# Block-causal attention, mixture of experts and feed-forward in one kernel: the probabilities of two heads laid side by side before they are transposed

## The chip, the cores and the metric

The kernel runs on one core of a Trainium2 chip, as one program. The metric is device time in microseconds (us) for the whole program. The core has a matrix engine (PE, with its weight loads listed apart as PEld), a vector engine (DVE), an activation engine (ACT), a general engine (POOL) and a queue that mostly issues transfers (SP). Each works through its own instructions in the order in which they are written, and waits on semaphores for the others.

## The reference

Three stages follow each other. In the first, scores are masked so that a row sees its own block of 64 keys and all earlier blocks:

```python
B, H, S, D = (4, 8, 576, 64)
scores = (1.0 / np.sqrt(D)) * np.matmul(q, k.transpose(0, 1, 3, 2))
mask = (pos[:, None] // 64) >= (pos[None, :] // 64)
scores = np.where(mask, scores, -1000000000.0)
attn = np.exp(scores - max);  attn = attn / (sum + 1e-09)
attn_out = np.matmul(attn, v)              # 32 heads of 576 x 64
x = attn_out, heads side by side           # 2304 tokens x 512
# moe: each token goes to the one expert of 8 with the largest logit x @ w_gate
out[mask] = gate_w * (np.maximum(x[mask] @ w1[e], 0) @ w2[e])     # 512 -> 1024 -> 512
# feed-forward: 512 -> 2048 -> 512 with softplus between
return softplus(x @ w_in) @ w_out
```

## The kernel before, in words

Everything is ordered by hand. One long string, `SCHEDULE`, lists short names, and the kernel calls what each name stands for, one after the other; that order is the order of instructions on every engine. A name such as `T10.3` means step `T10` of head pair 3. No scheduler moves anything afterwards.

**Attention** works on 16 head pairs (4 batches of 4 pairs). The 576 rows of a head are cut into chunk 0 (64 rows, 1 block) and chunks 1 to 4 (128 rows each, 2 blocks); chunk c sees 64(2c+1) keys. Per pair these steps occur:

- `Kt`, `Qt` (`prep_pe`, L331): K and Q of both heads are transposed on PE, four 128x128 blocks (`a`) and a fifth for the last 64 rows (`b`). `Kh`, `Qh` (ACT, L343) and `Kl`, `Ql` (DVE, L348) split the result into a high and a low part.
- `S0`, `S1`, `S2` (`scores`, L373): the score products. `m` (`s_max`, DVE, L383 and L381) masks a chunk and finds its extreme, `e` (`s_exp`, ACT, L388) takes the exponential and the row sum. `e41` is chunk 4 of head 1. Score tiles live in PSUM: chunk 4 has the one buffer of pool `ps2`, the others share the three banks of pool `pss` with `Kt` and `Qt`.
- `T` and `h` (`t_pe`, L394, and `t_out`, L399): the probabilities are transposed in 128x128 blocks, four to a bank of pool `ps1` (two banks), and copied to SBUF. `T11` is bank 1 of head 1. A head has 1, 2, 3, 4 and 5 blocks in its chunks, since a chunk's 64(2c+1) keys are padded to 128(c+1) with zeros: 15 blocks a head, 30 a pair, 480 in all. `h0x` and `h1x` are copied by ACT, `h2x` and `h3x` by DVE.
- `V` (`pv`, L409): the product with V, for each block of 128 keys once for each head. The two heads use the left and the right half of PE's columns. The fifth block of keys holds the last 64 rows of V twice, so that it works for either half.
- `F0`, `F1` (`o_out`), `Xa`, `Xb` (L424), `xa`, `xb`, `xo`: the result is turned back to rows, divided by the row sum, and stored; the same product gives the router's logits.

The steps of neighbouring pairs are interleaved: while pair 6 is scored, pair 5 is transposed and multiplied with V, and K and Q of pair 7 are prepared.

**Loads.** `f0`, `f1`, ... load the first batch head by head, `b1.0`, `b1.1`, ... the later batches. All but a few are issued by SP, and so are the stores `xo`, in the order of the string.

**After attention.** From the tenth pair on, DVE also works at the tables that say which token goes to which expert (`er`, the early routing). `wl0` to `wl7` load the first expert's weights, `h1x+0` (ACT) and `l1x+0` (DVE) split its first layer, `g0+0` and `g1+0` (POOL) fetch its tokens. Then come the experts' two layers, and the feed-forward. `lr` and `lg` are the late routing.

Of the kernel before, what the change touches and what calls it, by code (L numbers as in the profile page):

```python
# [54 lines left out]
Kla.1 e31.0 Qla.1 Ktb.1 Qtb.1 u4 e40.0 S1.0 Qhb.1 e01.0 Qlb.1 Khb.1 Klb.1 m30.0 S2.0 u5 m41.0 e30.0 m20.0 e41.0 m00.0
m10.0 e00.0 m21.0 S0.1 e20.0 m11.0 e10.0 e21.0 m40.1 T10.0 e11.0 T20.0 m31.1 h10.0 Kta.2 e40.1 h20.0 T00.0 Qta.2 m01.1
Kha.2 Xr.0 T31.0 h00.0 Kla.2 Qha.2 T21.0 h31.0 e31.1 Ktb.2 Qla.2 Qtb.2 T01.0 Qhb.2 e01.1 Qlb.2 Khb.2 S1.1 h21.0 h01.0
Klb.2 m30.1 S2.1 m41.1 e30.1 m20.1 T11.0 e41.1 m00.1 T30.0 m10.1 e00.1 m21.1 h11.0 m11.1 e20.1 h30.0 V.0 e10.1 e21.1
e11.1 Xr.1 F1.0 S0.2 F0.0 m40.2 T10.1 T20.1 m31.2 h10.1 Kta.3 e40.2 h20.1 T00.1 Qta.3 m01.2 Kha.3 T31.1 h00.1 Kla.3
Xa.0 Qha.3 h31.1 e31.2 Xb.0 Qla.3 T21.1 e01.2 xa.0 T01.1 xb.0 xo.0 b1.10 b1.11 f42 f43 f44 f45 f46 f47 b1.12 b1.13  # L60
b1.14 b1.15 b1.16 b1.17 Ktb.3 Qtb.3 h01.1 h21.1 S1.2 La.0 Qhb.3 Khb.3 Qlb.3 Klb.3 m30.2 S2.2 m41.2 e30.2 m20.2 T11.1
e41.2 m00.2 T30.1 m10.2 e00.2 m21.2 h11.1 m11.2 e20.2 h30.1 V.1 e10.2 e21.2 e11.2 Xr.2 F1.1 S0.3 F0.1 m40.3 T10.2 T20.2
m31.3 h10.2 Kta.4 e40.3 h20.2 T00.2 Qta.4 m01.3 Kha.4 T31.2 h00.2 Kla.4 Xa.1 Qha.4 h31.2 e31.3 Xb.1 Qla.4 T21.2 e01.3
xa.1 T01.2 xb.1 xo.1 Ktb.4 Qtb.4 h01.2 h21.2 S1.3 b2.0 La.1 b2.1 b2.2 b2.3 et Qhb.4 b2.4 b2.5 Khb.4 b2.6 b2.7 Qlb.4
b2.8 b2.9 Klb.4 b2.10 b2.11 m30.3 S2.3 m41.3 e30.3 m20.3 T11.2 e41.3 m00.3 T30.2 m10.3 e00.3 m21.3 h11.2 m11.3 e20.3
h30.2 V.2 e10.3 e21.3 e11.3 Xr.3 F1.2 S0.4 F0.2 m40.4 T10.3 T20.3 m31.4 h10.3 Kta.5 e40.4 h20.3 T00.3 Qta.5 m01.4 Kha.5
T31.3 h00.3 Kla.5 Xa.2 Qha.5 h31.3 e31.4 Xb.2 Qla.5 T21.3 e01.4 xa.2 T01.3 xb.2 xo.2 Ktb.5 Qtb.5 h01.3 h21.3 S1.4 La.2
Qhb.5 Khb.5 Qlb.5 Klb.5 m30.4 S2.4 m41.4 e30.4 m20.4 T11.3 e41.4 m00.4 T30.3 m10.4 e00.4 m21.4 h11.3 m11.4 e20.4 h30.3
V.3 e10.4 e21.4 e11.4 Xr.4 F1.3 S0.5 b2.12 F0.3 b2.13 b2.14 b2.15 b2.16 b2.17 m40.5 T10.4 T20.4 m31.5 h10.4 Kta.6 e40.5
# [1523 lines left out]
```

## Time and profile before

| | |
|---|---|
| median of 3 runs | 888.37 us (887.9 to 888.43) |
| the profiled execution's own time | 888.33 us |
| its span, first to last instruction | 886.6 us |
| PE busy | 869.0 us, 98% |
| PE's weight loads busy | 761.2 us, 86% |
| DVE busy | 671.1 us, 76% |
| ACT busy | 563.0 us, 63% |
| POOL busy | 128.0 us, 14% |

The shares are averages over very different stages. Attention takes roughly the first quarter of the span, the experts somewhat more, the feed-forward the rest. PE's work is pipelined: an instruction's listed length is the time it is under way, and the next begins before it has ended. What one costs in a stream is the distance from start to start.

### The profile page before, as it was taken

How to read it: one execution, taken by the hardware profiler on the slowest of the kernel's cores; microseconds unless marked ns; L12 is line 12 of the kernel's file. 1: busy time of each engine (PE TensorE's matmuls, PEld its weight loads, DVE VectorE, ACT ScalarE, POOL GpSimd, SP SyncE). 2: the span in 40 equal slices, each digit the busy share in tenths (PEclk: the TensorE clock that was granted, in tenths of full speed). 3: DMA queues.
4: the chain of work that ended last, by engine and by line, in shares of the span. 5: the costliest groups of instructions: out<-in, count | busy, mean ns of one | idle time of the engine just before them, and what ended most of it. 6: DMA issues, size and time to landing. Idle time of an engine off the chain costs nothing.

```text
span 886.6 us, 17835 instructions
## 1 busy us (share of the span) xinstructions
PE 869.0 (98%) x6037; PEld 761.2 (86%) x6037; DVE 671.1 (76%) x1627; ACT 563.0 (63%) x1252; POOL 128.0 (14%) x165
## 2 busy tenths in 40 slices
PE   8999999898999999999999999999999999999997
PEld 5788778676899899998998887888888999999997
DVE  6777788887899888765855568667775589897966
ACT  6676776676656667655855688878878734343332
POOL 1010000010022242211310100000000002241502
PEclk9999999999999999999999999999999999999999
DMA  5994734213516378966261567446765893434322
GB/s 122 186 208 83 140 87 142 90 52 122 162 67 211 117 238 282 314 224 224 76 226 48 178 212 229 163 167 219 281 224 202 250 320 109 155 122 141 127 89 96
DMA packets 139349, 148.63 MB, mean 168 GB/s; under 512 B 70895, under 2 KB 96495, under 8 KB 139248
## 3 DMA queue, kind: packets, MB, share of 16 engines
q1 hardware_dynamic: 132960, 132.24, 49.6%
q0 software_dynamic: 4800, 14.70, 4.8%
q8 instruction: 49, 0.80, 0.4%
q10 hardware_dynamic: 1488, 0.46, 0.2%
q14 instruction: 52, 0.43, 0.2%
HBM read 119.56 MB, written 41.43 MB: 182 GB/s over the span
## 4 chain that ended last, share of the span: by engine, by line
PE 63%; DVE 1%; DMA 1%; ACT 0%; issue 0%; SPq 0%; DVEq 0%; ACTq 0%
PE yps L1061 4%; PE yps L1063 3%; PE yps L1062 3%; PE fh L1204 3%; PE fh L1205 3%; PE fh L1203 3%; PE hps L1026 3%; PE hps L1027 3%; PE hps L1028 3%; PE fz L1370 3%; PE fz L1368 3%; PE fz L1369 3%; PE fX L1204 2%; PE fX L1203 2%; PE fX L1205 2%; PE fY L1204 2%
## 5 line engine op out<-in xcount | busy, mean ns | idle before, releaser
L1336 ACT CAST ah<-sum 128x1280 fp32r<-128x1280 f32 (+1 forms) x40 | 46.3, 1157 | 104.2 <-issue 44.7
L388 ACT ACTIVATE P<-s,negm 128x448 f32<-128x448 f32 (+4 forms) x160 | 82.8, 528 | 24.2 <-DVE negm L383 21.2
L1026 PE MATMUL hps<-xh,H1h 128*128 128x256 f32 x320 | 90.8, 284 | 0.0
L1028 PE MATMUL hps<-xh,H1l 128*128 128x256 f32 x320 | 90.5, 283 | 0.0
L1027 PE MATMUL hps<-xl,H1h 128*128 128x256 f32 x320 | 90.5, 283 | 0.0
L982 DVE TENSOR_TENSOR H2l<-R,H2h 128x512 fp32r<-128x512 f32 x96 | 63.7, 686 | 25.7 <-ACT H2h L978 25.7
L383 DVE CUSTOM_DVE_ANT_0 s<-s,mask 128x576 f32<-128x576 f32 (+3 forms) x128 | 69.3, 581 | 14.4 <-PE s L373 13.8
L978 ACT CAST H2h<-R 128x512 fp32r<-128x512 f32 x96 | 57.5, 624 | 29.7 <-PE yps L1062 14.3
L1401 POOL DMA_INDIRECT out_dram<-fos,OI x16 | 46.3, 2892 | 198.3 <-DVE fos L1393 162.5
L1061 PE MATMUL yps<-H2h,hh 128*128 128x512 f32 x176 | 71.5, 407 | 0.4 <-PEq L1533 0.4
L394 PE MATMUL pt<-ident,P 128*128 128x128 f32 x480 | 68.3, 278 | 3.5 <-DVE PT L399 2.5
L1062 PE MATMUL yps<-H2h,hl 128*128 128x512 f32 x176 | 68.8, 391 | 0.0
L1063 PE MATMUL yps<-H2l,hh 128*128 128x512 f32 x176 | 68.7, 391 | 0.0
L982 DVE TENSOR_TENSOR H1l<-R,H1h 128x512 fp32r<-128x512 f32 x96 | 62.2, 684 | 8.3 <-ACT H1h L978 6.2
L1340 DVE TENSOR_TENSOR al<-sum,ah 128x1280 fp32r<-128x1280 f32 (+1 forms) x40 | 54.1, 1352 | 17.4 <-ACT ah L1336 17.3
L978 ACT CAST H1h<-R 128x512 fp32r<-128x512 f32 x96 | 55.5, 623 | 16.0 <-PE hps L1027 10.3
L1026 PEld LDWEIGHTS hps<-xh,H1h 128*128 128x128 f32 x320 | 61.3, 192 | 0.5
L1027 PEld LDWEIGHTS hps<-xl,H1h 128*128 128x128 f32 x320 | 61.3, 192 | 0.3
L1028 PEld LDWEIGHTS hps<-xh,H1l 128*128 128x128 f32 x320 | 61.3, 192 | 0.0
L394 PEld LDWEIGHTS pt<-ident,P 128*128 128x128 f32 x480 | 52.6, 141 | 8.5 <-DVE PT L399 3.3
L409 PE MATMUL o<-PT,vraw 128*64 128x512 f32 (+4 forms) x384 | 59.1, 429 | 0.0
L373 PE MATMUL s<-kZ,qZ 64*128 64x288 f32 (+4 forms) x576 | 55.7, 312 | 3.5 <-DVE kZ L348 2.3
(361 smaller groups left out, 2603.9 us busy)
## 6 DMA issues: line engine op xcount, KB each, us to landing
R<-in_moe_w_dram SPq DMA_DIRECT2D x96, 512.0 KB
gd<-ft SPq DMA_DIRECT2D x64, 256.0 KB
gq<-gd SPq DMA_DIRECT2D x64, 256.0 KB
dbw<-in_moe_w_out_dram SPq DMA_DIRECT2D x32, 256.0 KB
dbl<-in_moe_w_in_dram SPq DMA_DIRECT2D x22, 256.0 KB
yg<-yd SPq DMA_DIRECT2D x4, 1026.0 KB
xd<-xs SPq DMA_DIRECT2D x16, 256.0 KB
wd<-ah SPq DMA_DIRECT2D x4, 896.0 KB
```

Of the source, the lines that this page charges most:

```text
L383: nc.vector.tensor_tensor_reduce(x, x, MASK[:, S - NK[c]:S], scale=1.0, scalar=3.0e38, op0=ALU.add, op1=ALU.min, accum_out=m)
L388: nc.scalar.activation(t[0:n, 0:NK[c]], SC.pop((p, j, c))[0:n], AF.Exp, bias=NM.pop((p, j, c))[0:n], scale=-1.0, accum_out=rs[p % 4][0:n, ...
L394: nc.tensor.transpose(ps[:, o:o + 128], P[p, j, c][:, 128 * kc:128 * kc + 128], ident)
L978: nc.scalar.copy(HW[l, i][0], raw(l, i))
L982: TT(l_, raw(l, i), h.bitcast(F32), op=ALU.subtract)
L1026: mm(a, lhsT=wh, rhs=xh, start=(k == 0), stop=False)
L1027: mm(a, lhsT=wh, rhs=xl, start=False, stop=False)
L1028: mm(a, lhsT=wl, rhs=xh, start=False, stop=(k == 3))
L1061: mm(o, lhsT=h[:, c], rhs=wh, start=(f == 0), stop=False)
L1062: mm(o, lhsT=l[:, c], rhs=wh, start=False, stop=False)
L1063: mm(o, lhsT=h[:, c], rhs=wl, start=False, stop=(f == 7))
L1204: mm(o, lhsT=wh[:, s], rhs=l, start=False, stop=False)
```

## The change

It has three parts.

1. **Probabilities of two heads side by side.** A chunk's tile now holds both heads, head 0's 64(2c+1) keys and then head 1's 64(2c+1), with head 1's blocks of 64 keys in reverse order (`s_exp` writes them so). Together that is 2c+1 whole blocks of 128 for a chunk, with no padding except in chunk 0. The middle one holds the last, unpaired block of 64 keys of both heads. A pair has 1+3+5+7+9 = 25 blocks to transpose. V of odd heads is loaded with the halves of each 128 rows swapped (`swapped`), and the unpaired blocks of V are loaded a second time into a tile `VZ` that has head 0's block in its upper left and head 1's in its lower right quarter and zeros elsewhere (`half_blocks`). `V` begins with four products with `VZ` for chunks 1 to 4, each for both heads in one, and one for chunk 0, and goes on with whole blocks, one for each head.
2. **One block for the last 64 rows of K and Q.** They are loaded into the upper and the lower half of one tile (`last_rows`), and `Ktb` transposes both; `Qtb` is gone. Loads of the last rows fall from 6 a batch to 2, and those of V grow in number (a later batch is 30 transfers where it was 18).
3. **A new order** of the whole attention part and of what lies beside it: the early routing, the first expert's loads, its token fetches and its conversions. From `V.15` on the two strings are the same, word for word.

The bank of the early routing moves from `ps2` to `ps1`, and the warm-up products at the start are 19 where they were 18.

```diff
-BANK = [
-    [(0, 1, 0), (0, 2, 128), (0, 3, 256), (0, 4, 384)],
...
-BW = [512, 512, 512, 320]
-NPB, PTB = 4, 4
+BANK = {
+    "00": [(0, 1, 0), (0, 2, 0), (0, 3, 0), (0, 4, 0)],
+    "10": [(1, 2, 0), (1, 3, 0), (1, 4, 0), (3, 4, 0)],
+    "20": [(2, 3, 0), (2, 4, 0), (2, 3, 1), (2, 4, 1)],
+    "21": [(c, c, None) for c in range(1, 5)],
+    "30": [(0, 0, None)],
+}
+for n in "01":
+    BANK[n + "1"] = [(kc, c, 1) for kc, c, _ in BANK[n + "0"]]
+NPB = 2
...
+    def last_rows(b, h0, nh):
+        t, i = raw[b, "k"], slice(h0, h0 + nh)
+        return [(t[r:r + 64, 4, i], x[b, i, 512:576, :].rearrange("h p d -> p h d")) for r, x in ((0, k), (64, q))]
+
+    def half_blocks(b, h):
+        o = slice(64 * (h % 2), 64 * (h % 2) + 64)
+        return VZ[b % 2][o, :, h // 2, o], v[b, h].rearrange("(n p) d -> p n d", p=64)[:, 0:9:2, :]
+
+    def swapped(b, h):
+        x = v[b, h].rearrange("(n p) d -> p n d", p=64)
+        return [(raw[b, "v"][64 * i:64 * i + 64, :, h], x[:, 1 - i:8:2]) for i in range(2)]
...
     def s_exp(p, j, c):
         n = SPAN[c][1]
-        t = P[p, j, c] = PB[(2 * p + j) % NPB][c]
-        nc.scalar.activation(t[0:n, 0:NK[c]], SC.pop((p, j, c))[0:n], AF.Exp, ...
+        t, x = PB[p % NPB][c][0:n, NK[c] * j:NK[c] * j + NK[c]], SC.pop((p, j, c))[0:n]
+        if j and c:
+            t, x = (a.rearrange("p (b k) -> p b k", k=64) for a in (t, x))
+            t = t[:, ::-1, :]
+        nc.scalar.activation(t, x, AF.Exp, ...
...
+    def t_pe(p, n):
+        if n == "30":
+            ps = PS[p, "E"] = pss.tile([128, 512], F32, tag="s", name="pt0")
+        else:
+            ps = PS[p, n] = ps1.tile([128, 512], F32, tag="ps1", name="pt")
+        for i, (kc, c, j) in enumerate(BANK[n]):
+            a = NK[c] + 64 + 128 * (c - 1 - kc) if j else 128 * kc
+            nc.tensor.transpose(ps[:, 128 * i:128 * i + 128], PB[p % NPB][c][:, a:a + 128], ident)
...
+        w = 64 if n == "30" else 512
+        (nc.scalar.copy if n in ("00", "01", "10") else nc.vector.tensor_copy)(t, ps[:, 0:w])
...
     def pv(p):
         b, hp = divmod(p, H // 2)
         o = PS[p, "o"] = pso.tile([128, 512], F32, tag="o", name="o")
-        o0 = PS[p, "o0"] = pss.tile([128, 512], F32, tag="s", name="o0")[:, 0:64]
-
-        for a, w, c, i, f in ((0, 512, 0, 0, 0), (0, 512, 1, 1, 0), (128, 384, 2, 2, 0), (384, 128, 4, 2, 384), (256, 256, 3, 3, 0), (None, 64, 0, 3, 256)):
+        o0 = PS[p, "o0"] = PS.pop((p, "E"))[:, 128:192]
+        for c in range(1, 5):
+            mm(o[:, 128 * c - 128:128 * c], lhsT=VZ[b % 2][:, c, hp], rhs=PT[p, "21"][:, 128 * c - 128:128 * c], start=c == 1, stop=False)
+        mm(o0, lhsT=VZ[b % 2][:, 0, hp], rhs=PT[p, "30"], start=True, stop=True)
+        for n, f, a, w, c in (("0", 0, 0, 512, 0), ("1", 0, 128, 384, 1), ("1", 384, 384, 128, 3), ("20", 0, 256, 256, 2)):
             for j in range(2):
-                out = (o0 if a is None else o[:, a:a + w])[64 * j:64 * j + 64]
-                mm(out, lhsT=raw[b, "v"][:, c, 2 * hp + j], rhs=PT[p, j, i][:, f:f + w], ...
+                r = PT[p, n][:, f + 256 * j:f + 256 * j + w] if n == "20" else PT[p, f"{n}{j}"][:, f:f + w]
+                mm(o[64 * j:64 * j + 64, a:a + w], lhsT=raw[b, "v"][:, c, 2 * hp + j], rhs=r, start=False, stop=c == 2)
...
-Xr.5 F1.4 S0.6 F0.4 m40.6 T10.5 T20.5 m31.6 h10.5 Kta.7 e40.6 h20.5 T00.5 Qta.7 m01.6 Kha.7 T31.5 h00.5 Kla.7 Xa.4
...
+e41.5 e10.5 S0.6 T20.5 F1.4 m40.6 F0.4 e21.5 Qta.7 e40.6 h20.5 Qha.7 T00.5 Kta.7 h00.5 Xa.4 Xb.4 m01.6 m31.6 T10.5
```

The new order is best seen on the engines. On PE, at the end of a steady period (pair 6), the last transposes and the product with V stand like this before; `pt` are transposes (P_0 and P_1 are tiles of probabilities, one set for a head), `o<-PT` products with V, 64x512 for one head.

```order
L394 MATMUL pt<-ident,P_1_129 128x128
L394 MATMUL pt<-ident,P_1_130 128x128
L394 MATMUL pt<-ident,P_1_131 128x128
L394 MATMUL pt<-ident,P_1_132 128x128
L394 MATMUL pt<-ident,P_0_126 128x128
L394 MATMUL pt<-ident,P_0_127 128x128
L394 MATMUL pt<-ident,P_0_123 128x128
L409 MATMUL o<-PT_1616,vraw 64x512
L409 MATMUL o<-PT_1652,vraw 64x512
L409 MATMUL o<-PT_1588,vraw 64x512
L409 MATMUL o<-PT_1714,vraw 64x512
L409 MATMUL o<-PT_1596,vraw 64x384
```

And now, at the same place (one set of P tiles for a pair):

```order
L420 MATMUL pt<-ident,P_0_126 128x128
L420 MATMUL pt<-ident,P_0_127 128x128
L420 MATMUL pt_1621<-ident,P_0_123 128x128
L433 MATMUL o<-PT_1603,VZ_134 128x128 x4
L434 MATMUL pt_1621<-PT_1625,VZ_134 128x64
L438 MATMUL o<-PT_1526,vraw 64x512
L438 MATMUL o<-PT_1619,vraw 64x512
L438 MATMUL o<-PT_1583,vraw 64x384
L438 MATMUL o<-PT_1623,vraw 64x384
L438 MATMUL o<-PT_1583,vraw 64x128
L438 MATMUL o<-PT_1623,vraw 64x128
L438 MATMUL o<-PT_1512,vraw 64x256 x2
```

Before, the four rows of P_1 at the top give PT_1714, which the fourth product reads; now five products with `VZ` stand between the last transposes and the first product with a half of PE's columns.

On ACT, at the same place of the same pair, these rows stood before (`P<-s` are exponentials, PT copies of transposed probabilities, xT the copy of V's result):

```order
L388 ACTIVATE P_2_136,rs_122<-s,negm 128x448
L388 ACTIVATE P_3_142,rs_122<-s_1657,negm 128x576
L388 ACTIVATE P_2_133,rs_122<-s,negm 64x64
L399 COPY PT_1714<-pt 128x512
L388 ACTIVATE P_2_135,rs_122<-s,negm 128x320
L388 ACTIVATE P_2_134,rs_122<-s,negm 128x192
L388 ACTIVATE P_3_140,rs_122<-s,negm 128x320
L388 ACTIVATE P_3_139,rs_122<-s,negm 128x192
L415 COPY xT_117<-o 128x512
```

And now:

```order
L410 ACTIVATE P_1_131,rs_122<-s,negm 128x448
L410 ACTIVATE P_1_128,rs_122<-s,negm 64x64
L426 COPY PT_1619<-pt 128x512
L410 ACTIVATE P_1_130,rs_122<-s,negm 128x320
L410 ACTIVATE P_1_129,rs_122<-s,negm 128x3x64
L410 ACTIVATE P_1_132,rs_122<-s_1567,negm 128x9x64
L410 ACTIVATE P_1_129,rs_122<-s,negm 128x192
L444 COPY xT_117<-o 128x512
L410 ACTIVATE P_1_130,rs_122<-s,negm 128x5x64
L410 ACTIVATE P_0_127,rs_119<-s_1657,negm 128x576
```

The exponential of chunk 4 of head 1 (128x576, now 128x9x64) was second and is sixth, the copy of PT is behind two exponentials where it was behind three, and the last exponential of the pair now stands behind the copy of V's result.

## Rows read from the trace of the kernel before

**Rows 1.** The page: the span, and each engine's busy time, share and instructions.

```profile
span 886.6 us, 17835 instructions
PE 869.0 (98%) x6037; PEld 761.2 (86%) x6037; DVE 671.1 (76%) x1627; ACT 563.0 (63%) x1252; POOL 128.0 (14%) x165
```

**Rows 2.** Busy time by stretch: length, busy us of each engine, granted clock, DMA.

```profile
24.80:128.90 104.10, 103.86 (x881) 85.10 (x880) 78.68 (x269) 73.52 (x233) 6.38 (x29) 1.00 0.75 147
76.90:89.90 13.00, 13.00 (x112) 10.60 (x110) 9.80 (x34) 9.20 (x30) 0.27 (x1) 1.00 0.12 30
128.90:221.50 92.60, 86.20 (x729) 67.99 (x727) 76.48 (x288) 64.08 (x197) 5.44 (x14) 1.00 0.30 97
142.70:171.30 28.60, 26.05 (x233) 20.87 (x232) 26.64 (x117) 18.75 (x59) 1.07 (x4) 1.00 0.39 132
221.50:886.60 665.10, 658.35 (x4282) 593.97 (x4280) 500.31 (x1024) 410.54 (x780) 112.07 (x85) 1.00 0.56 182
```

**Rows 3.** PE's instructions in time, pair 5: start, length, what, count.

```profile
84.49 1.39 PE L424 MATMUL psx<-xrhs,xT 128*128 128x144 f32 x10
85.72 1.04 PE L394 MATMUL pt<-ident,P 128*128 128x128 f32 x8
86.59 0.27 PE L331 MATMUL psT<-ident,kraw 128*128 128x128 f32 x1
86.90 2.24 PE L373 MATMUL s<-kZ,qZ 64*128 64x448 f32 x24
89.08 0.98 PE L394 MATMUL pt<-ident,P 128*128 128x128 f32 x7
89.99 3.88 PE L409 MATMUL o<-PT,vraw 128*64 128x512 f32 x24
93.79 0.48 PE L373 MATMUL s<-kZ,qZ 64*128 64x288 f32 x2
```

**Rows 4.** The product with V in time, ACT and PE's weight loads beside it.

```profile
90.47 1.02 PE L409 MATMUL o<-PT,vraw 128*64 128x512 f32 x3
90.76 0.57 ACT L399 COPY PT<-pt 128x512 f32<-128x512 f32 x1
90.90 1.13 PE L409 MATMUL o<-PT,vraw 128*64 128x512 f32 x3
91.38 0.19 PEld L409 LDWEIGHTS o<-PT,vraw 128*64 128x64 f32 x3 [0.34 <-ACT PT L399]
```

**Rows 5.** PE's groups by line, 60 to 140 us: busy, mean ns, idle before.

```profile
L394 PE MATMUL pt<-ident,P 128*128 128x128 f32 x188 | 26.6, 278 | 0.0
```

**Rows 6.** DVE's and ACT's groups by line, 63 to 141 us.

```profile
L399 DVE COPY PT<-pt 128x512 f32<-128x512 f32 x12 | 8.2, 681 | 0.0
L399 DVE COPY PT<-pt 128x320 f32<-128x320 f32 x12 | 5.8, 483 | 0.0
L413 DVE COPY xT<-o 128x64 f32<-128x64 f32 x6 | 1.3, 224 | 1.5 <-PE o L409 1.5
L388 ACT ACTIVATE P<-s,negm 128x192 f32<-128x192 f32 x12 | 5.0, 415 | 0.0
```

**Rows 7.** DVE in time: first and last step around seven extremes, and a small step.

```profile
93.39 0.22 DVE L429 RECIPROCAL rinv<-rinv 128x10 f32<-128x10 f32 x1
...
101.24 0.63 DVE L383 CUSTOM_DVE_ANT_0 s<-s,mask 128x448 f32<-128x448 f32 x1 [0.22 <-PE s L373]
...
104.32 0.49 DVE L399 COPY PT<-pt 128x320 f32<-128x320 f32 x1
```

**Rows 8.** ACT's groups by form, later stages: a read of every second element, a plain one.

```profile
L937 ACT ACTIVATE cvh<-dbl 128x256 f32<-128x256 f32 x18 | 7.2, 435 | 3.5 <-DMA dbl<-in_moe_w_in_dram 2.2 <-DVE cvl L938 1.4
L1213 ACT ACTIVATE ft<-fh 128x256 f32<-128x256 f32 x7 | 2.7, 381 | 2.9 <-PE fh L1205 1.8 <-DMA gd<-ft 1.0
```

**Rows 9.** SP's issues and ACT's first conversions in time.

```profile
43.76 6.36 SPq L291 DMA_DIRECT2D vraw<-in_v_dram  x6
193.81 1.14 ACT L978 CAST H1h<-R 128x512 fp32r<-128x512 f32 x2 [0.65 <-PE psT L331]
```

More of the change, by code (lines that the diff above doesn't have):

```diff
@@ L55 @@
[L55 to L69, printed above, removed]
@@ L286, in load_raw @@
             t = raw[b, nm]
+            g = slice(0, H, 2) if nm == "v" else slice(0, H)
             for c in range(4):
-                l.append((t[:, c], src[nm][b, :, 128 * c:128 * c + 128, :].rearrange("h p d -> p h d")))
-            for r in (0, 64):
-                l.append((t[r:r + 64, 4], src[nm][b, :, 512:576, :].rearrange("h p d -> p h d")))
+                l.append((t[:, c, g], src[nm][b, g, 128 * c:128 * c + 128, :].rearrange("h p d -> p h d")))
+            if nm == "k":
+                l += last_rows(b, 0, H)
+        for h in range(1, H, 2):
+            l += swapped(b, h)
+        l += [half_blocks(b, h) for h in range(H)]
         return [lambda o=o, i=i: nc.sync.dma_start(o, i) for o, i in l]
@@ L300, in attention @@
     rs = [const.tile([128, 5, 2], F32, name=f"rs{i}") for i in range(4)]
-    PB = [[const.tile([128, 128 * (c + 1)], F32, name=f"P{c}_{i}") for c in range(5)] for i in range(NPB)]
+    PB = [[const.tile([128, 2 * NK[c]], F32, name=f"P{c}_{i}") for c in range(5)] for i in range(NPB)]
+    VZ = [x.tile([128, 5, H // 2, 128], F32, name=f"VZ{i}") for i, x in enumerate((rawp, const))]
     def fill(t, v):
@@ L313, in attention @@
     start += [fillg(t[:, 576:640], 0.0) for t in xTp] + [fillg(t, 1.0) for t in rs]
-    for s in PB:
-        start += [fillg(s[0], 0.0)] + [fillg(s[c][:, 128 * c + 64:], 0.0) for c in range(1, 5)]
+    start += [fillg(s[0], 0.0) for s in PB]
+    start += [fillg(t, 0.0) for t in VZ]
     P, PS, PT, SC, NM, XS, Z = {}, {}, {}, {}, {}, {}, {}
@@ L321, in prep_pe @@
         b, hp = divmod(p, H // 2)
-        if part == "a":
-            ps = PS[p, nm] = pss.tile([128, 512], F32, tag="s", name="psT")
-            cs, off = range(4), 0
-        else:
-            if nm == "k":
-                PS[p, "4"] = pss.tile([128, 512], F32, tag="s", name="psT4")
-            ps, cs, off = PS[p, "4"], [4], {"k": 0, "q": 128}[nm] - 512
-        for c in cs:
+        ps = PS[p, nm if part == "a" else "4"] = pss.tile([128, 512], F32, tag="s", name="psT")
+        for i, c in enumerate(range(4) if part == "a" else [4]):
             t = raw[b, nm][:, c, 2 * hp:2 * hp + 2, :].rearrange("p h d -> p (h d)")
-            nc.tensor.transpose(ps[:, off + 128 * c:off + 128 * c + 128], t, ident)
+            nc.tensor.transpose(ps[:, 128 * i:128 * i + 128], t, ident)
     def prep_src(p, nm, part):
```

435 lines of the change are left out of this document (224 added, 211 removed), and 3 rows, old and new, of the table BANK.

## The prediction

> **What bounds the kernel now.** First the page: PE is busy 869.0 of the span of 886.6 us [rows 1]. Such a share says that PE is the engine to look at, not how much of its time is work, since the listed lengths overlap. So next the busy times by stretch, one for each stage [rows 2]. From the first product with V (24.8 us) to the ninth (128.9) eight pairs take 104.1 us, 13.0 each, and PE is idle for 0.24 us in all. A steady pair takes 13.00 us with PE busy 13.00, DVE 9.80 and ACT 9.20. In the next seven pairs (128.9 to 221.5) PE is idle for 6.4 of 92.6 us while DVE, which now has the routing beside attention, is busy 76.48; in its densest part, 142.7 to 171.3, it is busy 26.64 of 28.6, or 93%. From 221.5 on the two programs are the same; PE is idle there for 6.8 of 665.1 us. The granted clock is 1.00 (2.4 GHz) in all of them. So where the change acts, PE sets the pace, and for seven pairs DVE sets it with PE.
>
> Then PE's instructions in time, for what one costs [rows 3]. Eight transposes start at 85.72 and the next instruction at 86.59: 0.109 us each. The product with V starts at 89.99 and the scores behind it at 93.79: 3.80 us. Is that all work? One head's passes over 512 columns start 0.43 us apart (90.47, 90.90) [rows 4], there are two for each product, and the heads run side by side in the two halves. A head has 512+512+384+128+256+64 = 1856 columns, so 1856/512 x 2 x 0.43 = 3.12 us would do. The rest is mostly a wait: PE's weight loads stand idle until 91.38 behind ACT's copy of a PT tile, which runs from 90.76 to 91.33 [rows 4]. That is the copy behind three exponentials in the order on ACT. PE counts as busy meanwhile, since the other head's half is streaming: no idle time shows it.
>
> **The change, step by step.**
>
> *Transposes.* A pair loses 5 of 30 blocks of P, and one of its ten blocks of K and Q: 6 x 16 = 96. At 0.109 us each that is 0.65 us a pair, 10.5 us in all.
>
> The Trainium skill (TensorE: Matmul & The Clock Gate, Part 4: PE-mode transpose) puts a 128x128 transpose at about 275 ns in a kernel's context, and the trace's mean of one is indeed 278 ns [rows 5]. By that figure 96 would be 26.4 us. But 188 of them are busy for 26.6 us together [rows 5], half of what the mean would make, and in a stream the start-to-start price is what a removed one gives back.
>
> *The product with V.* The four `VZ` products have 128 columns in two passes, with weights over the whole array, which the trace has in two forms: transposes at 0.109, and `psx` with 144 columns at (85.72 - 84.49)/10 = 0.123 [rows 3]. Eight passes are 0.87 to 0.98; I take 0.9, nearer the transposes, which have the same width. Chunk 0's product is two passes of 64 columns, 0.05 each by columns, 0.109 if the weight load decides: 0.2 at most, taken. The whole blocks are 1280 columns a head: 1280/512 x 2 x 0.43 = 2.15. Together 3.25. The columns are as many as before; what goes is the wait: the last copies now have the 1.1 us of `VZ` products to be ready in, ACT's copy stands behind two exponentials, not three, and is needed second. Saved: 3.80 - 3.25 = 0.55 a pair (0 if a wait of the same size takes its place, 0.68 at most).
>
> *DVE and ACT.* DVE copies three tiles of 512 and one of 64 for two of 512 and two of 320: with 0.68, 0.22 and 0.48 [rows 6], -0.06 a pair. ACT loses one copy of 512. Four exponentials a pair are now written with blocks of 64 in reverse. No row has that; between nothing and the 0.05 us by which a read of every second element exceeds a plain one (435 against 381 ns [rows 8]): at most 0.2 a pair, on an engine with 3.8 us to spare.
>
> *The new order.* The next pair's `S0` needs the banks freed by the last exponentials. Between the end of `S1` and that `S0` PE does `S2` (half of 86.90 to 89.08: 1.09), nine transposes (0.98), the product with V (3.25) and a changeover (0.15): 5.5 us. In the same time DVE does the seven extremes of `S1` and `S2` (101.24 to 104.32 when they come in one run: 3.1 [rows 7]), two copies of 512 (1.36), one of 64 (0.22), and the two small steps of the reciprocal (0.2 each by [rows 7]): 5.1, and then ACT the last exponential, 0.42 [rows 6]: 5.5. That is a tie. Before, chunk 4's extreme came early and there was slack. So there may be a new wait of 0 to 0.5 us a pair at `S0`; I take 0.15, because most of ACT's and DVE's steps overlap at their ends.
>
> *Pairs 0 to 8.* Eight intervals, each shorter by 0.65 + 0.55 - 0.15 = 1.05: 8.4 us (5.2 without any gain at V, 9.6 without the new wait).
>
> *Pairs 9 to 15.* Here PE's own work would fall to 86.2 - 7 x 1.2 = 77.8 us, but DVE keeps 76.48 - 0.4 = 76.1. At the 93% that it reached in its densest part that takes 81.8 us; if only the transposes are felt, 92.6 - 7 x 0.65 = 88.0. The routing's steps are spread over more pairs now, which speaks for the lower figure, and the waits between the engines for the upper: I take 84.5, a gain of 8.1 (4.6 to 10.8).
>
> *The seam.* The first expert's conversions ran from 193.81 [rows 9] and are read only after the last product with V at 221.5: more than 20 us of cover. In the new order they are spread over the last two and a half pairs, the last some 10 us ahead of that point. Costed at nothing; if the cover were gone, one conversion would be about 0.6 us late.
>
> *Start.* The first scores now stand behind the second pair's K and Q, whose loads come later, but SP issues five transfers fewer before the first product with V, at about 1.06 us each (six in 6.36 us [rows 9]). Costed at 0, with 1 us either way. Behind `V.15` its own 0.5 is gained once more.
>
> *Sum.* 8.4 + 8.1 + 0.5 = 17.0. The profiled execution took 888.33 us, practically the median of the runs shown (888.37): 871.3 us.
>
> **Rivals.**
>
> *The wait moves.* The tie above goes the wrong way and `S0` waits 0.5 us in each pair, so that only the transposes are felt: 8 x 0.65 + 4 = 9.2, 879 us. For it: DVE and ACT have no slack left there. Against it: PE waits for an exponential nowhere in the steady pairs now.
>
> *Everything is had.* No new wait, and the routing's pairs at DVE's densest: 9.6 + 10.8 + 1 = 21.4, 867 us. Against it: 93% was reached over two pairs, not seven.
>
> *Slower: the chain through DVE and ACT becomes the bound.* In one pair it runs from `S0` through chunk 4's extreme and exponential, `Xa` and `Xb`, `S1`, DVE's 5.1 us and the last exponential back to `S0`. I count about 11.7 us for it, as for PE. From 13.0 on it costs more than the change gives, so its links would have to be 1.3 us longer than counted: a quarter of a microsecond at each of five hand-overs between engines. At 13.3 in 15 intervals, 892 us. Against it: every link but one is in today's order too, in 13.0 us with 3.2 us of DVE idle.
>
> *V comes late.* A later batch has 12 transfers more. Batch 1's last V load is issued by 50.1 [rows 9], and its first product starts at 76.9 [rows 2], 72.5 after the change. At 1.06 us each, 12 more end at 62.9: ten us to spare, nothing lost. At 2 us each and one after the other they would end 1.7 us late, three batches, 5 us: 876 us.
>
> The Trainium skill (SBUF - State Buffer, The DMA setup-cost knee) is on this rival's side: it gives every transfer a fixed cost of about 2 us and warns of many small ones. The trace has six in 6.36 us, so much of such a cost overlaps here.
>
> **How the numbers follow.** The forecast 0.55, the moved wait 0.24, everything 0.10, V late 0.04, slower 0.05, no change 0.02 (a wait that happens to eat it all). About 0.2% is what a measurement of this kernel tells from no change. Faster by more than that: 0.55 + 0.24 + 0.10 + 0.04 = 0.93; within it 0.02; slower 0.05. The range takes in the forecast, the moved wait and everything, with the bounds of the terms (17.0 may be 8.8 to 21.9): 866 to 880.
>
> **What would show it.** In the changed kernel's trace: 400 transposes of P where there were 480, still 0.109 apart; the product with V 3.2 to 3.4 us from its first start to the next scores, with no weight load waiting for a PT copy; steady pairs of 11.9 to 12.1 us with PE busy throughout; the seven pairs from the ninth product with V to the last in 82 to 88 us, DVE busy about 90%; the first product with V between 24 and 26 us; and 665 us from the last one on. Wrong would make it: PE idle before `S0` for an exponential (the moved wait), exponentials of chunk 4 in reverse much over 0.74 us, or PE idle before `V` for a load.

## The result, and the profile after

The changed kernel takes 877.78 us (median of 4 runs, 877.16 to 878.41) against 888.34 us for the kernel before: ratio 0.9882, 95% interval 0.9868 to 0.9896. That is faster by 10.6 us where 17 were forecast; the time lies inside the range. The profiled execution took 877.16 us, its span is 875.5 us.

The busy times by stretch of the changed kernel, cut at the same places as [rows 2] (first, fifth, sixth, ninth and last product with V); the columns are those of [rows 2]:

```profile
24.63:124.50 99.87, 99.33 (x849) 80.06 (x849) 76.90 (x266) 71.46 (x224) 6.40 (x29) 1.00 0.68 140
74.73:87.18 12.45, 12.37 (x107) 9.96 (x107) 9.62 (x34) 9.04 (x28) 0.27 (x1) 1.00 0.39 91
124.50:209.99 85.49, 83.12 (x703) 65.85 (x702) 75.32 (x287) 62.48 (x187) 6.08 (x14) 1.00 0.38 112
209.99:875.50 665.51, 658.06 (x4284) 594.40 (x4282) 500.17 (x1027) 410.76 (x780) 105.01 (x85) 1.00 0.56 184
```

The span fell by 11.1 us: 0.2 ahead of the first product with V, 104.10 - 99.87 = 4.2 in pairs 0 to 8, 92.60 - 85.49 = 7.1 in pairs 9 to 15, and 0.4 went back behind the last product. The seven pairs came out nearly as forecast (84.5). The eight steady ones did not: a pair takes 12.45 us, 0.55 less than before and not 1.05.

PE's instructions in time through one steady pair of the changed kernel (start, length, what, count), to be held against [rows 3]:

```profile
74.73 1.06 PE L433 MATMUL o<-PT,VZ 128*128 128x128 f32 x8
75.63 0.33 PE L434 MATMUL pt<-PT,VZ 128*128 128x64 f32 x2
75.89 2.37 PE L438 MATMUL o<-PT,vraw 128*64 128x512 f32 x16
78.20 1.13 PE L392 MATMUL s<-kZ,qZ 64*128 64x288 f32 x12
79.25 0.66 PE L420 MATMUL pt<-ident,P 128*128 128x128 f32 x4
...
81.15 1.49 PE L453 MATMUL psx<-xrhs,xT 128*128 128x144 f32 x10
82.48 1.04 PE L420 MATMUL pt<-ident,P 128*128 128x128 f32 x8
83.35 0.27 PE L350 MATMUL psT<-ident,kraw 128*128 128x128 f32 x1
83.55 2.22 PE L392 MATMUL s<-kZ,qZ 64*128 64x448 f32 x24
85.70 1.64 PE L420 MATMUL pt<-ident,P 128*128 128x128 f32 x9
87.18 1.06 PE L433 MATMUL o<-PT,VZ 128*128 128x128 f32 x8
```

Cut into pieces from start to start, with those of before out of [rows 3] (`S0` stands 13.00 ahead of 93.79 there, at 80.79):

| piece of a steady pair | before | after | difference |
|---|---|---|---|
| `S0` to `psx` (`S0` and 23, now 16 transposes) | 3.70 | 2.95 | -0.75 |
| `psx` | 1.23 | 1.33 | +0.10 |
| to `S1` (10, now 9 transposes) | 1.18 | 1.07 | -0.11 |
| `S1` and `S2` | 2.18 | 2.15 | -0.03 |
| to `V` (7, now 9 transposes) | 0.91 | 1.48 | +0.57 |
| `V` | 3.80 | 3.47 | -0.33 |
| sum | 13.00 | 12.45 | -0.55 |

Seven transposes left the piece from `S0` to `psx`, and it fell by what they cost, 7 x 0.109 = 0.76 us: in the kernel before PE's weight loads follow each other there without a gap. In the last piece it is otherwise. Nine transposes at 0.109 us are 0.98; between `S2` and `V` they take 1.48. PE's weight loads there say what they wait for (start, length, what, count; in brackets the idle time before and what ended it):

```profile
85.70 0.42 PEld L420 LDWEIGHTS pt<-ident,P 128*128 128x128 f32 x4
86.43 0.42 PEld L420 LDWEIGHTS pt<-ident,P 128*128 128x128 f32 x4 [0.31 <-DVE PT L426]
87.01 0.14 PEld L420 LDWEIGHTS pt<-ident,P 128*128 128x128 f32 x1 [0.16 <-ACT P L410]
```

The second four wait until DVE has copied the bank of four pairs of blocks (`h21`), the last one, chunk 0's, until ACT's exponentials have freed its bank. Now DVE and ACT of the same pair:

```profile
79.41 0.77 DVE L402 CUSTOM_DVE_ANT_0 s<-s,mask 128x576 f32<-128x576 f32 x1 [2.10 <-PE s L392]
80.26 0.74 ACT L410 ACTIVATE P<-s,negm 128x576 f32<-128x576 f32 x1 [0.79 <-DVE negm L402]
...
82.68 0.56 DVE L471 TENSOR_TENSOR xs<-psx,rinv 128x384 f32<-128x384 f32 x1 [0.27 <-PE psx L453]
...
84.89 0.22 DVE L400 TENSOR_REDUCE negm<-s 64x1 f32<-64x64 f32 x1 [0.25 <-PE s L392]
85.14 0.63 DVE L402 CUSTOM_DVE_ANT_0 s<-s,mask 128x448 f32<-128x448 f32 x1
...
85.95 0.64 ACT L410 ACTIVATE P<-s,negm 128x448 f32<-128x448 f32 x1 [1.47 <-DVE negm L402]
...
86.58 0.29 ACT L410 ACTIVATE P<-s,negm 64x64 f32<-64x64 f32 x1
```

Read with PE's rows, this is a ring. `S0` (78.20), chunk 4's extreme (79.41) and exponential (80.26), which frees the two banks for `psx` (81.15), DVE's multiplications of `psx` (82.68 to 83.78), which free them for head 1's half of `S1`, chunk 0's and chunk 3's extremes (84.89, 85.14), their exponentials (85.95, 86.58), chunk 0's transpose (87.01), `V` (87.18), and 3.47 us later the next `S0`. Each begins within about 0.2 us of the end of the one before. PE stands still at several places of that ring; the ring nowhere. That was the theory to be tested. Its rival: PE's own work fills the 12.45 us and the prices were wrong.

### The profile page after: what moved, and what is told of

Same layout as the page of the kernel before. It is cut to its first block, busy times and chain, and to the rows that moved or that the text cites. A ratio compares the mean times of both kernels' runs of the same rounds, so it can differ in the third digit from the quotient of the medians.

```text
span 875.5 us, 17767 instructions
## 1 busy us (share of the span) xinstructions
PE 861.2 (98%) x5974; PEld 754.4 (86%) x5974; DVE 667.5 (76%) x1627; ACT 559.6 (64%) x1236; POOL 124.2 (14%) x149
## 4 chain that ended last, share of the span: by engine, by line
PE 65%; DMA 1%; ACT 0%; SPq 0%; issue 0%; DVE 0%; DVEq 0%; ACTq 0%
PE yps L1090 4%; PE yps L1092 4%; PE yps L1091 3%; PE fh L1233 3%; PE fh L1234 3%; PE fh L1232 3%; PE hps L1056 3%; PE hps L1057 3%; PE hps L1055 3%; PE fz L1399 3%; PE fz L1397 3%; PE fz L1398 3%; PE fX L1233 2%; PE fX L1234 2%; PE fX L1232 2%; PE fY L1233 2%
## 5 line engine op out<-in xcount | busy, mean ns | idle before, releaser
L410 ACT ACTIVATE P<-s,negm 128x192 f32<-128x192 f32 (+4 forms) x160 | 83.6, 526 | 39.1 <-DVE negm L402 33.8
L402 DVE CUSTOM_DVE_ANT_0 s<-s,mask 128x576 f32<-128x576 f32 (+3 forms) x128 | 70.1, 569 | 26.4 <-PE s L392 23.5
L1430 POOL DMA_INDIRECT out_dram<-fos,OI x16 | 41.0, 2561 | 204.8 <-DVE fos L1422 166.5
L420 PE MATMUL pt<-ident,P 128*128 128x128 f32 x400 | 61.1, 281 | 2.1 <-DVE PT L426 0.8
L392 PEld LDWEIGHTS s<-kZ,qZ 64*128 64x128 f32 x576 | 47.3, 185 | 14.0 <-ACT P L410 5.5
L420 PEld LDWEIGHTS pt<-ident,P 128*128 128x128 f32 x400 | 44.3, 141 | 11.1 <-DVE PT L426 4.4
```

The costliest lines, as they stand in the source:

```text
L392: mm(o, lhsT=a, rhs=b, start=first, stop=last)
L402: nc.vector.tensor_tensor_reduce(x, x, MASK[:, S - NK[c]:S], scale=1.0, scalar=3.0e38, op0=ALU.add, op1=ALU.min, accum_out=m)
L410: nc.scalar.activation(t, x, AF.Exp, bias=NM.pop((p, j, c))[0:n], scale=-1.0, accum_out=rs[p % 4][0:n, c, j:j + 1])
L420: nc.tensor.transpose(ps[:, 128 * i:128 * i + 128], PB[p % NPB][c][:, a:a + 128], ident)
```

## Experiments

Each was timed beside the kernel before, whose median was 888.1 to 888.2 us there. All but the columns of time are from the profiled execution; the code behind the last product with V is the same in all, yet takes 663.7 to 669.3 us from that product to the end, so that small effects are read from the stretches and not from the total.

| run | median, us | ratio to before, 95% | first `V` | steady pair | pairs 0 to 8 | pairs 9 to 15 |
|---|---|---|---|---|---|---|
| before | 888.34 | | 24.80 | 13.00 | 104.10 | 92.60 |
| changed | 877.78 | 0.9868 to 0.9896 | 24.63 | 12.45 | 99.87 | 85.49 |
| e1 six more | 880.02 | 0.9887 to 0.9918 | 25.97 | 12.52 | 100.74 | 85.61 |
| e2 two more | 877.35 | 0.9862 to 0.9892 | 24.89 | 12.44 | 100.06 | 85.14 |
| e3 VZ last | 888.23 | 0.9991 to 1.0009 | 24.89 | 13.17 | 106.09 | 89.41 |
| e4 old places | 895.27 | 1.0060 to 1.0087 | 24.47 | 12.45 | 99.88 | 97.76 |
| e5 swap | 875.94 | 0.9850 to 0.9879 | 24.33 | 12.43 | 99.85 | 85.19 |
| e6 swap, copy on ACT | 876.05 | 0.9846 to 0.9875 | 24.98 | 12.44 | 99.85 | 84.50 |
| e7 old places behind `S0` | 888.17 | 0.9993 to 1.0011 | 24.35 | 12.45 | 99.89 | 96.52 |
| e8 before, early copy | 885.65 | 0.9969 to 0.9990 | 24.93 | 12.72 | 102.27 | 91.67 |
| e9 chunk 3 first | 873.48 | 0.9825 to 0.9852 | 24.25 | 12.26 | 98.57 | 84.22 |
| e10 and copy on ACT | 876.14 | 0.9856 to 0.9887 | 25.01 | 12.27 | 98.61 | 83.68 |
| e11 before, one block | 887.92 | 0.9994 to 1.0012 | 24.30 | 13.00 | 104.17 | 92.50 |
| e12 before, chunk 3 first | 885.93 | 0.9965 to 0.9986 | 24.89 | 12.83 | 103.13 | 91.54 |

**What the transposes were worth (e1, e2, e11).** e1 puts as many back as the change took away; they write the same blocks to the same places once more. e2 does it in bank 11 alone.

```diff
-        for i, (kc, c, j) in enumerate(BANK[n]):
+        for i, (kc, c, j) in [x for x in enumerate(BANK[n]) for _ in range(2 if n in ('20', '10', '11') and x[0] < 2 else 1)]:
```

> The changed kernel, but in three of a pair's seven banks (20, 10 and 11) the first two blocks are transposed twice into the same place: six transposes more a pair, as many as the change took away, 96 in all. At 0.109 us each that is 0.65 us a pair and 10.5 us. If PE alone sets the pace of the changed kernel, the steady pair goes from 12.45 to 13.1 us and the total rises by 10 to 10.5 us. If the steady pair is set by hand-overs from DVE and ACT (the changed kernel shows PE held up before the second bank of four transposes, before chunk 0's transpose and before psx, together about half a microsecond a pair), most of the six disappear in these waits: 12.5 to 12.8 us a pair, 1.5 to 5 us in total.

> The changed kernel, but in bank 11 alone, just ahead of the bank for which PE waits for DVE's copy, the first two blocks are transposed twice: 32 transposes more, 0.22 us a pair. If the wait is real, they are hidden in it: steady pair 12.45 to 12.5, total within 1 us of the changed kernel. If PE sets the pace: 12.67 us a pair and 3.5 us in total.

e1: 0.07 us in the steady pair, where 0.65 would be work; 2.2 us in total. Of these 1.3 stand ahead of the first product with V and are not the transposes' doing: in e1's trace the first of them starts at 19.03, and the delay is there by then, since PE ran at a granted clock of 0.50 from 15 to 18 us (1.00 in the changed kernel). The one of e1's four runs with a mean granted clock of 1.000 took 878.18 us. e2: nothing (12.44). In e1 the waits have gone into the transposes, as PE's instructions show: eleven of them behind `S2` take hardly longer than nine did, and `psx` and `S1` run without their waits.

```profile
83.18 1.39 PE L453 MATMUL psx<-xrhs,xT 128*128 128x144 f32 x10
84.41 1.25 PE L420 MATMUL pt<-ident,P 128*128 128x128 f32 x10
...
85.70 2.01 PE L392 MATMUL s<-kZ,qZ 64*128 64x448 f32 x24
87.64 1.68 PE L420 MATMUL pt<-ident,P 128*128 128x128 f32 x11
89.16 0.40 PE L433 MATMUL o<-PT,VZ 128*128 128x128 f32 x2
```

`psx` 1.23, `S1` and `S2` 1.94 (2.15 in the changed kernel), the last transposes 1.52. So the changed kernel has almost 0.6 us of room on PE in each steady pair.

e11 makes the second part of the change alone, in the kernel before: K's last 64 rows in the upper and Q's in the lower half of one tile, one transpose for both.

```diff
-        for r in (0, 64):
-            l.append((t[r:r + 64, 4, h0:h0 + nh], src[nm][0, h0:h0 + nh, 512:576, :].rearrange("h p d -> p h d")))
+        for r, x in ((0, nm), (64, "q" if nm == "k" else nm)):
+            l.append((t[r:r + 64, 4, h0:h0 + nh], src[x][0, h0:h0 + nh, 512:576, :].rearrange("h p d -> p h d")))
...
+        if nm + part == "qb":
+            return
```

> The kernel before with the second part of the change alone: the last 64 rows of K and Q in one block, one transpose less a pair (16 in all) and four transfers less a batch. By the start-to-start price of 0.109 us a steady pair goes from 13.00 to 12.89, the total down by 1.7 us (pairs 9 to 15 may keep theirs). By the mean duration of one, 0.278 us, it would be 4.4 us. If before, too, is held by hand-overs in the steady pair, nothing: within 0.5 us.

Nothing, neither in the steady pair nor in total. The transpose is gone, and what stands behind it has become longer by as much:

```profile
86.08 0.27 PE L335 MATMUL psT<-ident,kraw 128*128 128x128 f32 x1
86.28 2.35 PE L377 MATMUL s<-kZ,qZ 64*128 64x448 f32 x24
88.56 0.98 PE L398 MATMUL pt<-ident,P 128*128 128x128 f32 x7
```

0.20 us for the block of K instead of 0.31 for two [rows 3], then 2.28 for `S1` and `S2` instead of 2.18: `S1` waits for DVE to read `psx` in any case. So the kernel before had waits of PE too, though its PE is busy 13.00 us of 13.00 [rows 2]. This transpose stood behind `psx`, in front of such a wait; none was taken from the piece between `S0` and `psx` alone, where PE has no wait.

**The product with V (e3, e8).** e3 puts the products with `VZ` and chunk 0's behind the whole blocks.

```diff
-        for c in range(1, 5):
-            mm(o[:, 128 * c - 128:128 * c], lhsT=VZ[b % 2][:, c, hp], ..., start=c == 1, stop=False)
-        mm(o0, lhsT=VZ[b % 2][:, 0, hp], rhs=PT[p, "30"], start=True, stop=True)
         for n, f, a, w, c in (("0", 0, 0, 512, 0), ...
...
-                mm(o[64 * j:64 * j + 64, a:a + w], ..., start=False, stop=c == 2)
+                mm(o[64 * j:64 * j + 64, a:a + w], ..., start=n == "0", stop=False)
+        for c in range(1, 5):
+            mm(o[:, 128 * c - 128:128 * c], lhsT=VZ[b % 2][:, c, hp], ..., start=False, stop=c == 4)
+        mm(o0, lhsT=VZ[b % 2][:, 0, hp], rhs=PT[p, "30"], start=True, stop=True)
```

> The changed kernel with the products of V in another order: the whole blocks of 128 keys first, the four products with VZ and chunk 0's last. Same instructions, no cover for the last copies of PT. If the products with VZ are what hides ACT's last copy, V grows by 0.4 to 0.6 us a pair (3.47 to 3.9 to 4.1) and the total by 6 to 9 us. If the order within V does not matter, because the steady pair waits elsewhere anyway, less than 1.5 us.

`V` grows from 3.47 to 4.10 us (91.47 to 95.57 below) and the pair from 12.45 to 13.17. The whole blocks take 2.85 us where they took 2.31; PE's weight loads stand idle for 0.35 us among them, until 92.02, behind ACT's copy of a PT tile. All of the change's gain is gone: 888.23 us is the time of before. That it is the same time is chance: pairs 0 to 8 are slower than before (106.09 for 104.10), pairs 9 to 15 still faster (89.41 for 92.60).

```profile
91.47 2.91 PE L435 MATMUL o<-PT,vraw 128*64 128x512 f32 x16
94.32 1.16 PE L437 MATMUL o<-PT,VZ 128*128 128x128 f32 x8
95.31 0.33 PE L438 MATMUL pt<-PT,VZ 128*128 128x64 f32 x2
95.57 0.67 PE L392 MATMUL s<-kZ,qZ 64*128 64x288 f32 x5
```

e8 shortens the wait in the kernel before: ACT's copy of bank 1 of head 1 goes one exponential up.

```diff
-... T11.7 e41.8 m00.8 T30.7 m10.8 e00.8 m21.8 h11.7 m11.8 e20.8 h30.7 V.7
+... T11.7 e41.8 m00.8 T30.7 m10.8 h11.7 e00.8 m21.8 m11.8 e20.8 h30.7 V.7
```

> The kernel before, but ACT's copy of bank 1 of head 1 (the PT tile for which the product with V waits in the middle) stands ahead of chunk 0's exponential, behind two exponentials where it stood behind three. Nothing else changes. If the product with V of before holds a wait of half a microsecond for that copy, which no idle time shows, its length goes from 3.80 to 3.45 to 3.6 us and the total down by 2.5 to 5 us. If the length is work, or another copy is as late, less than 1 us.

`V` 3.52 us, 0.28 less than before, and the pair 12.72, 0.28 less:

```profile
89.05 3.59 PE L409 MATMUL o<-PT,vraw 128*64 128x512 f32 x24
92.57 1.12 PE L373 MATMUL s<-kZ,qZ 64*128 64x288 f32 x12
```

The hidden wait in `V` was real, and what is taken from `V` comes back in full: `V` is a link of the ring in the kernel before.

**The other links (e5, e6, e9, e10, e12).** e5 swaps two neighbours on DVE, from pair 3 on:

```diff
-... Klb.8 h10.6 m00.7 m30.7 S2.7 h21.6 T11.6 ...
+... Klb.8 h10.6 m30.7 m00.7 S2.7 h21.6 T11.6 ...
```

e6 does the same and takes `h21` to ACT:

```diff
-... Klb.8 h10.6 m00.7 m30.7 S2.7 h21.6 T11.6 ...
+... Klb.8 h10.6 h21.6 m30.7 m00.7 S2.7 T11.6 ...
...
-        (nc.scalar.copy if n in ("00", "01", "10") else ...
+        (nc.scalar.copy if n in ("00", "01", "10", "21") else ...
```

> The changed kernel, but from pair 3 on DVE takes the extreme of chunk 3 of head 0 ahead of that of chunk 0 (two neighbours on one engine change places, nothing else). Theory: a steady pair is a closed chain without slack, S0, chunk 4's extreme and exponential, psx, its two multiplications on DVE, S1, the extremes of chunks 0 and 3, their exponentials, chunk 0's transpose, V, S0: its links add up to the 12.45 us. The swap takes the 0.25 us of chunk 0's extreme out of the chain, but PE's wait for DVE's copy of bank 21 then ends last, 0.10 to 0.15 us earlier than now: steady pair 12.30 to 12.37, total 1 to 2 us down. If PE's own work is what fills the 12.45 us: no change (within 0.5 us).

> As the swap of chunk 3's and chunk 0's extremes, and the copy of bank 21 is done by ACT, right behind that of bank 10, and no longer by DVE. Neither PE's wait for that copy nor chunk 0's extreme is then in the way of the last transposes. Theory of the closed chain: 0.2 to 0.3 us a pair, steady pair 12.15 to 12.25, and DVE has 0.68 us less in each of the routing's pairs: total 3 to 5 us below the changed kernel. If another link takes over at once: less than 1 us.

Both failed to move the steady pair (12.43, 12.44). ACT and DVE of e5 show why:

```profile
84.59 0.63 DVE L402 CUSTOM_DVE_ANT_0 s<-s,mask 128x448 f32<-128x448 f32 x1 [0.26 <-PE s L392]
...
85.31 0.22 DVE L400 TENSOR_REDUCE negm<-s 64x1 f32<-64x64 f32 x1
...
85.65 0.63 ACT L410 ACTIVATE P<-s,negm 128x448 f32<-128x448 f32 x1 [1.47 <-DVE negm L400]
```

The exponential of chunk 3 now waits for chunk 0's extreme (L400), the later of the two: they share one score tile. The link is as long as it was, so neither run speaks against the ring. e6 removes PE's wait for `h21` all the same, and chunk 0's transpose then waits the longer for ACT: that wait lay beside the ring, not on it. Where the routing loads DVE, the copy on ACT seems to help: pairs 9 to 15 took 84.50 (85.19 in e5), in one profile each.

e9 shortens that link itself. In `S1` the passes of head 0 (chunks 3 and 0) alternate with those of head 1 (chunk 4), and head 1's first waits for `psx` to be read. Head 0 goes two ahead; the instructions are the same.

```diff
+        if u == 1:
+            lists[1][:0] = [None, None]
         for i in range(max(map(len, lists))):
             for l in lists:
-                if i < len(l):
+                if i < len(l) and l[i]:
```

> The changed kernel, but in S1, where the passes of head 0 (chunks 3 and 0) and of head 1 (chunk 4) alternate on PE, head 0's passes stand two ahead. Same instructions. Why the swap of the two extremes changed nothing in the steady pair: ACT's exponential of chunk 3 still waited for the later of the two extremes, so that link of the chain stayed as long as it was. This edit shortens the link itself: head 1's first pass waits about 0.37 us for the bank that DVE's multiplications of psx free, and head 0's passes no longer stand behind it. Theory of the closed chain: chunk 3 and chunk 0 are complete 0.2 to 0.35 us earlier, and the steady pair, all of whose other links are untouched, goes from 12.45 to 12.1 to 12.25 us; total 2.5 to 5 us below the changed kernel. If PE's own work is the bound, or another chain of the same length stands beside this one: within 0.05 us a pair.

> As head 0's passes two ahead in S1, and the copy of bank 21 on ACT right behind that of bank 10. If, once the chain is shorter, PE's wait for DVE's copy of bank 21 is the next to end last, this gives 0.05 to 0.15 us a pair more (steady pair 12.0 to 12.15); if not, the steady pair is that of the other run, and only the routing's pairs, where DVE has 0.68 us less each, gain 0.5 to 2 us.

e9: 12.26 us a pair, 0.19 less, and 873.48 us, faster than both kernels. Of the 4.3 us below the changed kernel 2.6 lie in the fifteen intervals (1.3 each in pairs 0 to 8 and 9 to 15); the rest lies ahead of them, behind them, or between the profiled execution and the median. The extremes come 1.16 us behind `S1`'s start (83.74 and 82.58 below) where they came 1.34 behind it (84.89 and 83.55 above), and DVE, which had waited 0.25 us for them, waits no more. That bounds the gain.

```profile
82.58 2.22 PE L394 MATMUL s<-kZ,qZ 64*128 64x448 f32 x24
...
83.45 0.21 DVE L367 SCALAR_TENSOR_TENSOR kZ<-psT,kZ 128x64 fp32r<-128x64 f32 x1
83.74 0.21 DVE L402 TENSOR_REDUCE negm<-s 64x1 f32<-64x64 f32 x1
```

e10: the same pair, 12.27; the copy of bank 21 is not next on the ring. Its seven pairs are shorter by 0.5 us, but it began 0.8 us later, and its median is 2.7 us above e9's; the rest of that is not explained.

e12 makes the same edit in the kernel before.

> The kernel before, with head 0's passes two ahead in S1, as in the faster variant of the changed kernel; same instructions. One transpose less a pair was worth nothing in the kernel before, so its steady pair, too, should be a chain through DVE and ACT and not PE's work: S1, chunk 3's extreme, three exponentials, the copy of PT, the second half of the product with V, the next S0. If so, V's wait for that copy becomes 0.15 to 0.3 us shorter, the steady pair goes from 13.00 to 12.7 to 12.85 us and the total down by 2 to 4 us. If PE's own work sets the 13.00 us: within 0.5 us.

`V` 3.63 us, 0.17 less, and the pair 12.83, 0.17 less: there, too, a ring, through `S1`, the exponentials and ACT's copy.

```profile
89.55 3.70 PE L411 MATMUL o<-PT,vraw 128*64 128x512 f32 x24
93.18 1.06 PE L375 MATMUL s<-kZ,qZ 64*128 64x288 f32 x11
```

**The places of the routing (e4, e7).** e4 keeps attention's new order and puts `er`, `wl`, `g`, `h1x`, `l1x` and the next expert's loads behind the attention steps behind which they stood before, but leaves them in one order among themselves. That brings many of them elsewhere: `Xr.11`, early between `V.10` and `V.11` in the kernel before, is the last step ahead of `V.11` in the new order, and the 17 steps from `er43` to `er54`, spread over the interval before, now stand in one block between the two. e7 moves those that then stand between a `V` and the next `S0` behind that `S0`. Around `S0.11`, e4 against the changed kernel, and e7 against e4:

```diff
-V.9 m11.10 e20.10 m41.10 er14 e11.10 m21.10 m10.10 e41.10 e10.10 S0.11 T20.10 F1.9 er15 er16 ...
+V.9 m11.10 e20.10 m41.10 e11.10 m21.10 er7 er8 er9 er40 er10 er41 m10.10 e41.10 e10.10 er11 er42 er12 S0.11 T20.10 F1.9 ...
```

```diff
-... m21.10 er7 er8 er9 er40 er10 er41 m10.10 e41.10 e10.10 er11 er42 er12 S0.11 T20.10 ...
+... m21.10 m10.10 e41.10 e10.10 S0.11 er7 er8 er9 er40 er10 er41 er11 er42 er12 T20.10 ...
```

> The changed kernel with attention's new order, but the early routing, the first expert's loads, fetches and conversions put back behind the attention steps behind which they stood before. Pairs 0 to 8 stay at 12.45 us. If the new places are worth something of their own, the stretch from the ninth product with V to the last goes from 85.5 to 88 to 90 us, and the total up by 2.5 to 4.5 us. If the seven pairs gained only by the new layout and attention's order, less than 1 us.

> The run with the routing's steps at their old places cost 17.5 us. Here the same old places, but those of the steps that stand between a product with V and the next S0 are moved just behind that S0; which pair they fall in stays as it was. Theory: they cost that much because they stand on DVE ahead of extremes whose exponentials free the banks that S0 waits for, a link of the closed chain. Then the stretch from the ninth product with V to the last comes back from 97.8 to 86 to 89 us, the total to 878 to 882. If it is the crowding into fewer pairs that costs, it stays above 890.

Both expectations were far off. e4: 97.8 us for the seven pairs, worse than the 92.6 of before. (Another 4 us were lost behind the last product with V, where PE once stood idle for 3.4 us.) e7: 96.5; moved behind `S0`, the steps gave back 1.2 us, so it was hardly their place ahead of `S0` that cost. Their number alone is not it either: between `V.10` and `V.11` stand 34 of the routing's steps in e4 and e7, 31 in the kernel before, 13 in the changed one, and that interval takes 19.5, 21.0, 15.4 and 12.6 us. Here it is in e7 (columns as above):

```profile
151.44:172.40 20.96, 15.48 (x119) 11.64 (x119) 17.15 (x76) 10.02 (x31) 0.54 (x2) 0.92 0.46 160
```

PE is busy 15.5 of 21.0 us and DVE 17.2: the routing's small steps on DVE and its products on PE wait for each other in turn (PE 2.8 us for a table of DVE's, DVE 2.0 us for a product of PE's), and attention's steps queue behind them. The wait of 2.8 us stands right ahead of `V.11`, in the block of 17 steps that neither e4 nor e7 took away from there (e4 has it too, up to 171.73). From the last nine transposes to `V.11` it is 4.6 us in e4, 5.3 in e7 and 1.45 in the changed kernel. The clock also fell in both (last section). So the two runs show that blocks of the routing's steps in front of `V` are dear, and not what the old places as such would cost. What part of the 7.1 us belongs to the new places and what to the layout was not separated.

## Why the prediction was right, and where it was not

- **Pairs 0 to 8: -8.4 forecast, -4.2 measured**, below the lower bound of 5.2. Here the prediction failed, and in its first step: "where the change acts, PE sets the pace". A steady pair was, and is, a ring through three engines. PE's busy 13.00 us of 13.00 contains the waits, since lengths overlap; the prediction said so of `V` and did not ask it of the rest. Two of its signs failed with it: a steady pair of 11.9 to 12.1 us and a `V` of 3.2 to 3.4. That the total lies inside the range all the same is in part luck: the range's lower end sums the lower bounds of both stretches, and pairs 9 to 15 stayed 2.5 us above theirs (4.6).
- **Transposes: -0.65 a pair.** The price of 0.109 us from start to start is right where PE does not wait, and the seven that left the piece between `S0` and `psx` gave it back. But it is not "what a removed one gives back" everywhere: in the changed kernel six put back cost 0.07 us (e1), and one taken from the kernel before in front of a wait gave nothing (e11). So the transposes' 0.65 became work that is gone and, for the most part, waits in its place (below). The Trainium skill (TensorE: Matmul & The Clock Gate, Part 4: PE-mode transpose) gives about 275 ns for one, an estimate of 26.4 us for 96. With e1 putting 96 back for 2.2 us by the medians, the runs bear out neither price as what a transpose is worth here.
- **`V`: 3.80 to 3.25 forecast, 3.47 measured.** The wait and its cover are right (e3, e8). The size is not: the `VZ` products took 0.90 as forecast, but chunk 0's product with the changeover behind it 0.26 (0.2), and the whole blocks 2.31 (2.15), of which 0.1 is the changeover to `S0` that the sum had left out.
- **The new wait at `S0`: 0.15.** There is none at `S0`. It came elsewhere: the last transposes now hold 0.50 us beyond their 0.109 each (0.15 before: 0.91 for seven), and `psx` 0.10. The first is the wait for DVE's and ACT's copies and exponentials ahead of `V`, the second the one for chunk 4's exponential. So 0.65 + 0.55 - 0.15 = 1.05 became 0.65 + 0.33 - 0.35 - 0.10 = 0.53, with 0.03 from the scores 0.56; measured 0.55.
- **Rivals.** The measured time is nearest to the wait that moves (879): right in size, wrong in place. The slower rival named a ring through DVE and ACT, and the way from `S0` through chunk 4 and `psx` to `S1` is that of the true one. The rest of its way, DVE's seven extremes and the last exponential back to `S0`, did not bind; what bound was chunk 3's and chunk 0's exponentials, chunk 0's transpose and `V`. It counted 11.7 us for its ring; the true one takes 12.45.
- **Pairs 9 to 15: -8.1 forecast, -7.1 measured.** PE's idle time there fell from 6.4 to 2.4 us, DVE is busy 88% (90% forecast). A part can be named: without the cover of the `VZ` products these pairs take 89.4 us (e3), so 3.9 of the 7.1 us hang on it. The rest is not taken apart.
- **Behind the last `V`: -0.5 forecast, +0.4 measured.** In the last pair no exponential stands in front of ACT's copy, so `V.15` had no wait to lose. It shows the work of each form: 3.28 us before (221.54 to 224.82) and 3.46 after. The other 0.2 us are within what this stretch varies by.

```profile
221.54 3.35 PE L409 MATMUL o<-PT,vraw 128*64 128x512 f32 x24
224.82 1.09 PE L1000 MATMUL t<-ident,xg 128*128 128x128 f32 x8
```

```profile
209.99 1.06 PE L433 MATMUL o<-PT,VZ 128*128 128x128 f32 x8
...
213.45 1.09 PE L1029 MATMUL t<-ident,xg 128*128 128x128 f32 x8
```

The first fence is PE of the kernel before, the second of the changed one. So `VZ` costs 0.18 us of work a pair and saves a wait of 0.5.
- **Start, loads, seam, reversed writes: nothing, as forecast.** The first product with V stands at 24.63 (24.80 before), none waits for a load of V, and chunk 4's exponential takes 0.74 us straight (80.26 above) and in reverse (at 76.61) alike.

## What to carry to other kernels

Where an order is written by hand and buffers are few, an engine that is busy all the time need not be the bound: follow one period from release to release round all engines, and price only what lies on that ring. To see whether work on the busy engine matters at some place, put more of it in there: if the time stays, taking it out of there will hardly help. An edit pays when it shortens a link: a few words that let one half of `S1` run ahead (e9) brought 2.6 us more in the attention's pairs, beside the 11.3 that the whole rearrangement brought there.
